# A linear-attention and mixture-of-experts kernel: float32 products on unsplit operands in the attention

## The chip, the cores and the metric

The kernel runs on one core of one Trainium2 chip. The metric is the device time of one execution in microseconds (us); runs of the same kernel here lie within 0.2% of each other.

## The reference, cut to what matters

Three layers in a row, all in float32 (the dense weights arrive as float64 words and are narrowed on the chip):

```python
# attention with a decaying state, 4 batches x 8 heads x 768 tokens x 40 dimensions
m_new = max(f[t] + m, i[t]); f_stab = exp(f[t] + m - m_new); i_stab = exp(i[t] - m_new)
C = f_stab * C + i_stab * outer(v[t], k[t]);  n = f_stab * n + i_stab * k[t]
y[t] = sigmoid(o_gate[t]) * (C @ q[t]) / max(abs(n . q[t]), 1)
x = y as [3072 tokens, 320]
# dense layer: 320 -> 2048 -> 320, leaky relu
x = max(0.01 * (x @ w_in), x @ w_in) @ w_out
# experts: the best of 8 by x @ w_gate, 320 -> 1024 -> 320, times its gates
out[token] = gate[token] * eom[token] * (relu(x @ w1[e]) @ w2[e])
```

The attention is computed in chunks of 128 tokens. Within a chunk the scores (key by query) are multiplied by a matrix of decays; those "probabilities" times v (with a column of ones beside it, 41 columns) give the chunk's own part. The state of 40 x 41 for each head carries the earlier chunks.

## The kernel before, in words

A **unit** is one chunk of one batch with all 8 heads; there are 24, and `unit(i)` emits one as a generator that yields between its stages. In a unit:

1. The raw q, k, v of 128 tokens arrive in `raw` (float32). q and k are split into float16 parts, a high part by ACT's copy and a remainder, and transposed by DMA. For units in `QG` Pool scales q and k in place first and forms the remainder.
2. The decays `gm` (float32) come from TensorE (units 0 to 5) or from a broadcast load with exponentials on ACT (from unit `PEU` = 6 on).
3. For all but the last chunk Pool forms `wv`, v times its weight towards the state; ACT rounds it to float16 (`wvh`) and Pool forms the remainder (`wvl`).
4. v itself is rounded by ACT (`vh`), its remainder is DVE's (`vl`).
5. For each half of the heads four score matmuls fill the one PSUM buffer of tag "S" (L762), DVE multiplies it into `gm`, Pool (ACT for units in `PA`) rounds the product to float16 (`ph`, L768), and Pool (DVE for `LV`) forms the remainder (`pl`).
6. `pv` (L782 to L784) has three float16 matmuls for each head: high times high, high times low, low times high.
7. DVE normalises the result; the gates (`XG`: on Pool, else DVE) and the rounding of x into two float16 parts by `pack` follow (the remainders on Pool for units in `PG`, else on DVE), and a DMA transposes x into `xT`.
8. After each second batch `state` adds both batches' k times `wv` into PSUM (L852: three float16 products for each head and batch, 48 for a pair of units) and updates the state, of which `C3` is a split copy for the next chunk.

**The dense layer** runs in 96 steps, interleaved with the units from about 48 us on: 16 matmuls of 256 columns (L903), ACT and DVE form the leaky relu, ACT and Pool split it into `gh` and `gl`, and 12 matmuls of 320 columns follow (L925 to L927) two steps later. **The experts** follow the last dense step, in blocks of 128 tokens.

**What sets the order.** Each stage has a planned time (`UNITS`, `OFF`, `TICKS`). The class `Order` runs a list schedule by those times, with a cost for each instruction, and fixes the order of the instructions on every engine up to planned time 350. The times are not waited for on the chip: an engine takes its next instruction as soon as the instruction's inputs and its buffer are there, and whatever stands behind a waiting instruction on the same engine waits too. SP issues the loads and the transposes, in order as well. `Bufs` hands scratch buffers round: a load into one waits until its last reader is out. The large weight conversions of the dense layer (`narrow`, `split`: on DVE, ACT and Pool) lie between the first eight units.

Of the kernel before, what the change touches and what calls it, by code (L numbers as in the profile page):

```python
# [20 lines left out]
C = 128  # L21
# [7 lines left out]
PF = 10                      # pairs of tiles from here on share the dense weights' last pass  # L29
TA = 2 * PF                  # token tiles of the first dispatch  # L30
NBA = TA - E + 1             # full blocks that TA tiles always hold
NBH = E // 2                 # first blocks of the rest: up to half a block of two experts each
NBB = NBH + NTILE + E // 2 - 1 - NBA    # blocks of the rest, at most
# [3 lines left out]
S_V = 2.0 ** 5  # L37
S_C = 2.0 ** -4
S_N = 2.0 ** 15
# [25 lines left out]
class Slots:  # L65
    """a tile pool whose tags keep the order of their tiles"""
# [13 lines left out]
class Order:  # L80
    """the order of every engine's instructions: a list schedule by planned time"""
# [61 lines left out]
    def run(self, instrs, planned, pools):  # L143
# [49 lines left out]
        wait = {e: [] for e in self.ENGINES}     # (ready time, i)  # L193
        avail = {e: [] for e in self.ENGINES}    # (priority, i)
# [98 lines left out]
class Bufs:  # L293
    """buffers in turn, each free again once its last reader is out"""
# [12 lines left out]
# the plan: times of the units, of their stages, of the dense steps and of the weights' loads and splits  # L307
UNITS = [2.7, 0, 19, 17.2, 28.8, 32, 42.5, 46.5]
UNITS += [16 + 2.87 * i for i in range(16)]      # from the ninth on in ticks
# [20 lines left out]
# units whose decay between tokens the tensor engine adds up  # L330
PEU = 6
# what the Pool engine takes from the vector engine: packs, reciprocals times gates, gates from these chunks on,
# remainders of queries and keys, of weights
PG = {3, 15, 23}
XG = {0, 2, 5, 8}
# [3 lines left out]
# units whose weights the scalar engine rounds; whose remainders the vector engine takes  # L339
PA = {3, 4, 6}  # L340
LV = {4}
# weights that the scalar engine scales; units with one transpose for query and key
WA = {(2, 0)}
MT = set()
# where blocks begin that few inputs use
RARE = [26, 28]
# the last planned time of a fixed order; lead and queue of the loads
# [5 lines left out]
def emit(tc, gates, qkv, og, w_in, w_out, w_gate, w1, w2, out):  # L353
# [23 lines left out]
    # arena views  # L377
# [44 lines left out]
    maskb = cp.tile([128, C], BF, name="maskb")      # -1e30 where the key is behind the query  # L422
# [47 lines left out]
    def narrow(r):  # L470
        """float64 words -> float32"""
        n = r.shape[1]
        cv = cv64()
        a, b = (x[:, 0:n] for x in cv)
        lo, hi = r[:, :, 0], r[:, :, 1]
        V.tensor_scalar(out=a, in0=hi, scalar1=3, scalar2=0x3FFFFFF8, op0=ALU.logical_shift_left,
                        op1=ALU.bitwise_and)
        yield 0.35
        stt(V, b, hi, -0x40000000, a, ALU.bitwise_and, ALU.bitwise_or)
        yield 0.65  # L480
        stt(V, a, lo, 29, b, ALU.logical_shift_right, ALU.bitwise_or)
        return a.bitcast(F32), cv

    def piece_win(j, blk, lead):
# [8 lines left out]
        else:  # L493
            # two column blocks' last rows: the remainders of each on the other half of the partitions
# [29 lines left out]
    def piece_w2(e, k0, n, until=0.0):  # L524
        """until: the time at which what lay there is used"""
# [24 lines left out]
    raw_r = Bufs([R.f32(2 * DM + H * D1) for _ in range(3)], "raw_r")  # L550
    QK = Bufs([R.f16(2, H, 128) for _ in range(4)], "QK")
    QKT = Bufs([R.f16(2 * H, 128) for _ in range(2)], "QKT")
    VH = Bufs([R.f16(H, 42) for _ in range(2)], "VH")
    VL = Bufs([R.f16(H, 42) for _ in range(2)], "VL")
    GM = Bufs([R.f32(H, C) for _ in range(3)], "GM")
    PH = Bufs([R.f16(4, C) for _ in range(4)], "PH")
    PL = Bufs([R.f16(4, C) for _ in range(4)], "PL")
    WV = Bufs([R.f32(H, D1) for _ in range(2)], "WV")
    WVH = Bufs([R.f16(H, 42) for _ in range(3)], "WVH")
    WVL = Bufs([R3.f16(H, 42) for _ in range(3)], "WVL")  # L560
# [26 lines left out]
    def parts(c):  # L587
        """g and b of chunk c as a sum of three bfloat16 parts, one on each group of 32 partitions"""
# [9 lines left out]
    def arguments(c, h0, tag):  # L598
        """g of the query + b of the key, masked, of four heads: [key, head, query]"""
# [15 lines left out]
    def emit_gates(c0, c1):  # L615
        """gates of chunks c0 to c1: g and b by token, decay of the chunk"""
# [33 lines left out]
        outs = [(gw, wT, S_V)]  # L650
# [19 lines left out]
    def emit_sig(c):  # L670
        """output gates of two chunks"""
        for n in range(2):
            sg[c + n] = SG()
            SP.dma_start(sg[c + n], og[c + n])
        yield SGD
        for n in range(2):
            A.activation(out=sg[c + n], in_=sg[c + n], func=AF.Sigmoid)
            ready.add(c + n)
# [8 lines left out]
    def unit(i):  # L687
        """one (batch, chunk) of all heads"""
# [18 lines left out]
        if i in QG:  # L707
            scaled(G, raw[:, 0:2 * DM], S_QK)
# [12 lines left out]
        else:  # L721
            for a, x in ((qt, qr), (kt, kr)):
                SP.dma_start_transpose(out=a, in_=x.rearrange("p h d -> p (h d)"))
        if i >= PEU:
# [15 lines left out]
        if c < NC - 1:  # L740
            wv, wvh, wvl = WV(), WVH(), WVL()
# [3 lines left out]
            yield 0.7  # L745
            copy(wvh[:, :, 0:D1], wv)
            yield 0.3
            less(True, wvl[:, :, 0:D1], wv, wvh[:, :, 0:D1])
            WV.free(wv)
            st[c, b] = (kr, wvh, wvl, qk)  # L750
        yield to("v")
        vh, vl = VH(), VL()
        copy(vh[:, :, 0:D1], v, S_V)
        low(vl[:, :, 0:D1], v, S_V, vh[:, :, 0:D1])
        raw_r.free(raw)
        pp = []
        for hf in range(2):
# [6 lines left out]
            ph, pl = PH(), PL()  # L764
            if i in PA:
                copy(ph, p32)
            else:
                G.tensor_scalar(out=ph, in0=p32, scalar1=1.0, scalar2=0.0, op0=ALU.mult, op1=ALU.add)  # L768
            yield 0.5
            less(not (i in LV), pl, p32, ph)  # L770
            if hf:
                GM.free(gm)
            pp.append((ph, pl))
# [4 lines left out]
        def pv(hf):  # L778
            ph, pl = pp[hf]
            for h in range(4):  # L780
                g = 4 * hf + h
                T.matmul(o1[:, g, :], ph[:, h, :], vh[:, g, 0:D1], start=True, stop=False)  # L782
                T.matmul(o1[:, g, :], ph[:, h, :], vl[:, g, 0:D1], start=False, stop=False)
                T.matmul(o1[:, g, :], pl[:, h, :], vh[:, g, 0:D1], start=False, stop=True)  # L784

        yield to("p")
        pv(0)
        pv(1)
        PH.free(pp[0][0], pp[1][0])
        PL.free(pp[0][1], pp[1][1])  # L790
        VH.free(vh)
        VL.free(vl)
# [36 lines left out]
        if c == NC - 1:  # L829
            QK.free(qk)  # L830
# [14 lines left out]
    def state(c, pr):  # L845
        up = ps.tile([128, H, D1], F32, tag="aux", name="up", bufs=3)
        for h in range(H):
            for m in range(3):
                for n, o in ((0, 0), (1, 64)):
                    kr, wvh, wvl, _ = st[c, 2 * pr + n]  # L850
                    k0, k1 = ((0, 64), (80, 128), (0, 64))[m] if n == 0 else ((0, 40), (80, 120), (0, 40))[m]
                    T.matmul(up[o:o + k1 - k0, h, :], kr[:, h, k0:k1], (wvh, wvh, wvl)[m][:, h, 0:D1],  # L852
                             start=(m == 0), stop=(m == 2))
        for n in range(2):
            QK.free(st[c, 2 * pr + n][3])
            WVH.free(st[c, 2 * pr + n][1])
            WVL.free(st[c, 2 * pr + n][2])
# [37 lines left out]
    def gemm1(xT, n, kp):  # L895
        """two feed-forward tiles: their leaky relu, split"""
# [54 lines left out]
    late = []           # for the logits of the last tiles, behind the first blocks of experts  # L951

# [1 line left out]
    def routing():  # L954
# [21 lines left out]
        half = [rt([128, E], F32, f"half{i}") for i in range(2)]      # block and row of an expert's half  # L976
# [12 lines left out]
        def dispatch(first, bufs, R1, RS, group):  # L989
            """slots of the blocks: their rows, tokens, scales and experts"""  # L990
# [23 lines left out]
            # scale  # L1014
# [9 lines left out]
            # rank in the expert  # L1024
# [22 lines left out]
            # blocks of the experts  # L1047
# [28 lines left out]
            # block of every token, out of the way for those that the other dispatch holds  # L1076
            def of_expert(i, a, r):
                """a of the expert of every token"""
# [8 lines left out]
            if not first:  # L1087
                # behind the full blocks: half a block
# [9 lines left out]
            # slot -> token  # L1098
# [23 lines left out]
            # row c * 512 + b * 128 + p is token b * 768 + c * 128 + p; none beyond the last  # L1122
# [52 lines left out]
        def experts(q):  # L1175
            """rows of the block and their expert: one for all or a fixed one for each half"""
# [42 lines left out]
        def chain(q0, q1, ahead):  # L1219
            """blocks q0 to q1, each one's second product after the next one's first"""  # L1220
# [105 lines left out]
    for j in range(4):  # L1326
        # these lie where the dense weights of steps up to t lay: two pieces of w_in, then w_out
# [76 lines left out]
```

## Time and profile before

| | us |
|---|---|
| median of 3 runs (lowest, highest) | 726.77 (726.21, 727.49) |
| span of the profiled execution, first to last instruction | 721.0 |
| median less span | 5.8 |
| PE, DVE, ACT, POOL busy | 596.5, 486.8, 369.6, 391.2 |

The page gives only the span for the profiled execution, so its own time is taken as the span and the 5.8 us that the median of the runs lies above it. PE is TensorE's matmuls, PEld its weight loads, DVE VectorE, ACT ScalarE, POOL GpSimd, SP the engine that issues most DMAs. A matmul's recorded duration is a latency: matmuls overlap, so what one costs in a stream is read from the distance of starts.

### The profile page before, as it was taken

What the parts mean: (1) busy time and instruction counts of PE and PEld (TensorE: products, weight loads), DVE (VectorE), ACT (ScalarE), POOL (GpSimd) and SP (SyncE); (2) the same over time, 40 slices, a digit from 0 to 9 for tenths busy, and PEclk for the clock granted to TensorE, in tenths of its full rate; (3) what the DMA queues carried; (4) which work ended last, traced back from release to release, by engine and by line L of the source; (5) the groups of instructions that cost most, each with busy time, mean ns of one, the idle gap of its engine ahead of it and who ended that gap; (6) DMA issues with size and microseconds to landing.
All of it is one profiled execution on the core that took longest, in us unless ns stands there. A gap on an engine that the chain in (4) does not pass through costs nothing. (4 is left out here: it accounts for less than half of the span.)

```text
span 721.0 us, 15741 instructions
## 1 busy us (share of the span) xinstructions
PE 596.5 (83%) x5624; PEld 426.0 (59%) x5624; DVE 486.8 (68%) x871; ACT 369.6 (51%) x772; POOL 391.2 (54%) x392
## 2 busy tenths in 40 slices
PE   3447779769787788977898899999699999999894
PEld 1235557547666566756676687776455655665552
DVE  7999999995588789779698876688635722122110
ACT  5546464677665676777655566655332222222220
POOL 6867887466866858867665544524523422223111
PEclk9997999999999999989999999999899999999997
DMA  8686893681957796987666656544599877777632
GB/s 226 228 150 85 184 259 111 209 215 27 186 159 159 211 237 123 228 185 178 136 161 153 170 153 193 155 129 129 165 198 180 160 155 131 159 151 154 148 88 50
DMA packets 215081, 116.77 MB, mean 162 GB/s; under 512 B 170011, under 2 KB 202523, under 8 KB 215004
## 3 DMA queue, kind: packets, MB, share of 16 engines
q1 hardware_dynamic: 212092, 106.68, 64.6%
q0 software_dynamic: 2912, 9.05, 4.5%
q8 instruction: 50, 0.82, 0.5%
q14 instruction: 27, 0.22, 0.1%
HBM read 64.58 MB, written 9.06 MB: 102 GB/s over the span
## 5 line engine op out<-in xcount | busy, mean ns | idle before, releaser
L903 PE MATMUL hp<-xT,arena 128*128 128x256 f16 x1536 | 197.2, 279 | 8.8 <-DVE g L366 7.8
L366 POOL TENSOR_TENSOR gl<-g,gh 128x512 f16<-128x512 f32 x96 | 131.8, 1374 | 111.1 <-ACT gh L375 108.7
L903 PEld LDWEIGHTS <-arena 128*128 128x128 f16 x1536 | 148.3, 100 | 31.5 <-issue 5.7
L925 PE MATMUL acc<-arena,gh 128*128 128x320 f16 x384 | 117.3, 307 | 14.3 <-DVE arena L1276 4.8
L927 PE MATMUL acc<-arena,gl 128*128 128x320 f16 x384 | 117.1, 308 | 9.9 <-POOL gl L366 9.8
L366 POOL TENSOR_TENSOR arena<-arena 128x512 f16<-128x512 f32 (+5 forms) x94 | 111.2, 1195 | 18.5 <-ACT arena L375 10.2
L926 PE MATMUL acc<-arena,gh 128*128 128x320 f16 x384 | 117.4, 306 | 0.5 <-POOL arena L366 0.5
L363 DVE SCALAR_TENSOR_TENSOR r<-hp,r 128x512 f16<-128x512 f32 x52 | 35.9, 691 | 120.8 <-ACT r L1194 106.5
L363 DVE SCALAR_TENSOR_TENSOR arena<-arena 128x328 f16<-128x328 f32 (+7 forms) x113 | 99.1, 888 | 9.3 <-ACT arena L375 7.1
L1188 PE MATMUL hp<-arena,xbb 128*128 (+1 forms) x480 | 95.5, 382 | 5.9 <-issue 5.6
L375 ACT ACTIVATE gh<-g 128x512 f16<-128x512 f32 x96 | 60.1, 626 | 70.3 <-DVE g L366 67.6
L366 DVE TENSOR_TENSOR g<-hp,t 128x512 f32<-128x512 f32 x96 | 65.2, 680 | 41.6 <-ACT t L375 36.0
L1207 PE MATMUL y<-arena,rT 128*128 (+1 forms) x720 | 90.4, 299 | 0.8 <-DMA rT<-r 0.5
L375 ACT ACTIVATE arena<-arena 128x328 f16<-128x328 f32 (+5 forms) x128 | 72.9, 599 | 33.3 <-DVE arena L363 12.7
L1207 PEld LDWEIGHTS <-rT 128*128 128x128 f16 (+1 forms) x720 | 61.8, 101 | 28.0 <-DMA rT<-r 1.4
L1211 POOL DMA_INDIRECT out<-ys,si x26 | 26.8, 1030 | 90.2 <-ACT ys L1210 83.3
L1188 PEld LDWEIGHTS <-xbb 128*128 128x128 f16 (+1 forms) x480 | 41.5, 102 | 53.1 <-issue 10.7
L375 ACT ACTIVATE t<-hp 128x512 f32<-128x512 f32 x96 | 56.1, 585 | 30.0 <-PE hp L903 29.9
L363 DVE SCALAR_TENSOR_TENSOR arena<-stg,arena 128x960 f16<-128x960 f32 (+3 forms) x48 | 57.5, 1198 | 15.3 <-ACT arena L375 14.9
L1194 ACT ACTIVATE r<-hp 128x512 f16<-128x512 f32 x52 | 31.0, 597 | 65.5 <-PE hp L1188 49.3
L375 ACT ACTIVATE arena<-stg 128x1024 f16<-128x1024 f32 (+2 forms) x48 | 46.9, 978 | 17.6 <-DMA stg<-w 10.6
L1169 POOL DMA_INDIRECT xbb<-x2rows,gi x26 | 28.0, 1077 | 49.0 <-PE hp L1188 42.9
(242 smaller groups left out, 855.3 us busy)
## 6 DMA issues: line engine op xcount, KB each, us to landing
stg<-w SPq DMA_DIRECT2D x24, 512.0 KB
arena<-qkv SPq DMA_DIRECT2D x24, 484.0 KB
arena<-gd SPq DMA_DIRECT2D x18, 512.0 KB
stg<-w SPq DMA_DIRECT2D x16, 480.0 KB
raw<-w_in SPq DMA_DIRECT2D x10, 512.0 KB
arena<-w_out SPq DMA_DIRECT2D x8, 640.0 KB
x2rows<-x2r SPq DMA_DIRECT2D x24, 192.0 KB
arena<-og SPq DMA_DIRECT2D x6, 640.0 KB
```

Of the source, the lines that this page charges most:

```text
L363: eng.scalar_tensor_tensor(out=o, in0=a, scalar=s, in1=b, op0=op0, op1=op1)
L366: eng.tensor_tensor(out=o, in0=a, in1=b, op=op)
L375: A.activation(out=o, in_=a, func=AF.Copy, scale=s)
L903: T.matmul(hp[:, kk, :], win_v[:, j, wb, o:o + 128], xT[:, xb, :], start=(m == 0), stop=(m == 7))
L925: T.matmul(acc[i], gh[:, kk, r], wh, start=(k == lo), stop=False)
L926: T.matmul(acc[i], gh[:, kk, r], wl, start=False, stop=False)
L927: T.matmul(acc[i], gl[:, kk, r], wh, start=False, stop=(k == hi))
L1169: G.indirect_dma_start(out=xb, out_offset=None, in_=rows, in_offset=bass.IndirectOffsetOnAxis(ap=gi[:, i:i + 1], axis=0), bounds_check=(TA ...
L1188: T.matmul(hp[n][r], xT[:, xb, r], W1v[:, e, wb, n * 512:(n + 1) * 512].rearrange("p a b -> p (a b)"), start=(m == 0), stop=(m == 7))
L1194: A.activation(out=r[:, 0, :], in_=hp[n], func=AF.Relu)
L1207: T.matmul(y[r], a[:, r], W2v[:, e, k, m, :].rearrange("p a b -> p (a b)"), start=(k + n == 0), stop=(k == 7 and n == 2))
L1211: G.indirect_dma_start(out=out, out_offset=bass.IndirectOffsetOnAxis(ap=D_[s][1][:, i:i + 1], axis=0), in_=ys, in_offset=None, bounds_chec ...
```

## The change

The float16 splits of the probabilities, of v and of the weighted v go away; the products that used them become one float32 matmul for each head. k for the state is taken from the raw load, so `raw` lives until the state's product and q and k may no longer be scaled in place (`QKS` takes the scaled copy). Pool takes the gates (`XG`) and the remainders of x (`PG`) of all units. Scales and numbers of buffers follow. The planned times stay as they are.

```diff
-S_V = 2.0 ** 5
-S_C = 2.0 ** -4
-S_N = 2.0 ** 15
+S_W = 2.0 ** 5
+S_C = 2.0
+S_N = S_QK * S_QK
-PG = {3, 15, 23}
-XG = {0, 2, 5, 8}
+PG = set(range(24))
+XG = set(range(24))
-PA = {3, 4, 6}
-LV = {4}
...
-    raw_r = Bufs([R.f32(2 * DM + H * D1) for _ in range(3)], "raw_r")
-    QK = Bufs([R.f16(2, H, 128) for _ in range(4)], "QK")
+    raw_r = Bufs([R.f32(2 * DM + H * D1) for _ in range(6)], "raw_r")
+    QKS = R.f32(2 * DM)
+    QK = Bufs([R.f16(2, H, 128) for _ in range(2)], "QK")
...
-    GM = Bufs([R.f32(H, C) for _ in range(3)], "GM")
-    PH = Bufs([R.f16(4, C) for _ in range(4)], "PH")
-    PL = Bufs([R.f16(4, C) for _ in range(4)], "PL")
-    WV = Bufs([R.f32(H, D1) for _ in range(2)], "WV")
-    WVH = Bufs([R.f16(H, 42) for _ in range(3)], "WVH")
-    WVL = Bufs([R3.f16(H, 42) for _ in range(3)], "WVL")
+    GM = Bufs([R.f32(H, C) for _ in range(4)], "GM")
+    WV = Bufs([R.f32(H, D1) for _ in range(4)], "WV")
...
         if i in QG:
-            scaled(G, raw[:, 0:2 * DM], S_QK)
+            G.tensor_scalar(out=QKS, in0=raw[:, 0:2 * DM], scalar1=S_QK, scalar2=0.0, op0=ALU.mult, op1=ALU.add)
+            q, k = (QKS[:, u * DM:(u + 1) * DM].rearrange("p (h d) -> p h d", h=H) for u in range(2))
...
+        QK.free(qk)
...
-            wv, wvh, wvl = WV(), WVH(), WVL()
+            wv = WV()
             tt(G, wv, v, w.to_broadcast([128, H, D1]), ALU.mult)
-            yield 0.7
-            copy(wvh[:, :, 0:D1], wv)
-            yield 0.3
-            less(True, wvl[:, :, 0:D1], wv, wvh[:, :, 0:D1])
-            WV.free(wv)
-            st[c, b] = (kr, wvh, wvl, qk)
-        yield to("v")
-        vh, vl = VH(), VL()
-        copy(vh[:, :, 0:D1], v, S_V)
-        low(vl[:, :, 0:D1], v, S_V, vh[:, :, 0:D1])
-        raw_r.free(raw)
+            st[c, b] = (raw, wv)
...
             tt(V, p32, sc, p32, ALU.mult)
-            ph, pl = PH(), PL()
-            if i in PA:
-                copy(ph, p32)
-            else:
-                G.tensor_scalar(out=ph, in0=p32, scalar1=1.0, scalar2=0.0, op0=ALU.mult, op1=ALU.add)
-            yield 0.5
-            less(not (i in LV), pl, p32, ph)
...
-                T.matmul(o1[:, g, :], ph[:, h, :], vh[:, g, 0:D1], start=True, stop=False)
-                T.matmul(o1[:, g, :], ph[:, h, :], vl[:, g, 0:D1], start=False, stop=False)
-                T.matmul(o1[:, g, :], pl[:, h, :], vh[:, g, 0:D1], start=False, stop=True)
+        for h in range(H):
+            T.matmul(o1[:, h, :], gm[:, h, :], v[:, h, :], start=True, stop=True)
+        GM.free(gm)
+        if c == NC - 1:
+            raw_r.free(raw)
...
         for h in range(H):
-            for m in range(3):
-                for n, o in ((0, 0), (1, 64)):
-                    kr, wvh, wvl, _ = st[c, 2 * pr + n]
-                    k0, k1 = ((0, 64), (80, 128), (0, 64))[m] if n == 0 else ((0, 40), (80, 120), (0, 40))[m]
-                    T.matmul(up[o:o + k1 - k0, h, :], kr[:, h, k0:k1], (wvh, wvh, wvl)[m][:, h, 0:D1],
-                             start=(m == 0), stop=(m == 2))
+            for n, o in ((0, 0), (1, 64)):
+                raw, wv = st[c, 2 * pr + n]
+                k0 = DM + h * D
+                T.matmul(up[o:o + 64 - 24 * n, h, :], raw[:, k0:k0 + 64 - 24 * n], wv[:, h, :], start=True, stop=True)
```

## Rows read from the trace of the kernel before

**Rows 1.** Busy time by stage, columns: stretch, length, engines (instructions), clock, DMA.
```profile
0.00:162.00 162.00, 104.85 (x1071) 75.73 (x1072) 151.42 (x228) 92.74 (x190) 115.77 (x134) 0.94 0.75 186
162.00:414.00 252.00, 210.64 (x2448) 166.81 (x2447) 199.21 (x329) 167.04 (x387) 173.75 (x164) 0.97 0.71 165
414.00:522.70 108.70, 99.87 (x855) 77.94 (x852) 80.48 (x159) 62.44 (x107) 49.31 (x41) 0.98 0.54 155
522.70:721.00 198.30, 181.16 (x1260) 105.47 (x1258) 55.65 (x156) 47.43 (x89) 52.32 (x54) 0.97 0.72 143
```
**Rows 2.** DVE's groups by line, 0 to 162 us: busy us, mean ns | idle before.
```profile
L363 DVE SCALAR_TENSOR_TENSOR arena<-arena 128x328 f16<-128x328 f32 x9 | 7.0, 776 | 0.2
...
L366 DVE TENSOR_TENSOR arena<-arena,rd 128x320 f32<-128x320 f32 x5 | 4.9, 988 | 0.1
L363 DVE SCALAR_TENSOR_TENSOR xr<-arena,xr 128x256 f16<-128x256 f32 x7 | 3.7, 524 | 0.0
...
L363 DVE SCALAR_TENSOR_TENSOR xr<-arena,xr 128x128 f16<-128x128 f32 x7 | 3.1, 437 | 0.0
```
**Rows 3.** DVE's groups by line, 162 to 414 us.
```profile
L363 DVE SCALAR_TENSOR_TENSOR arena<-arena 128x328 f16<-128x328 f32 x15 | 12.1, 805 | 1.7 <-ACT arena L375 1.7
...
L363 DVE SCALAR_TENSOR_TENSOR xr<-arena,xr 128x256 f16<-128x256 f32 x14 | 11.6, 829 | 4.4 <-ACT xr L375 4.4
...
L366 DVE TENSOR_TENSOR arena<-arena,rd 128x320 f32<-128x320 f32 x14 | 9.5, 681 | 0.2
...
L363 DVE SCALAR_TENSOR_TENSOR xr<-arena,xr 128x128 f16<-128x128 f32 x14 | 8.0, 569 | 1.7 <-ACT xr L375 1.6
```
**Rows 4.** Groups by line of the whole span, POOL's.
```profile
L366 POOL TENSOR_TENSOR arena<-arena 128x512 f16<-128x512 f32 x48 | 63.9, 1337 | 2.7 <-ACT arena L375 1.1
...
L768 POOL TENSOR_SCALAR arena<-arena 128x512 f16<-128x512 f32 x42 | 30.4, 724 | 15.3 <-DVE arena L366 14.5 <-DVE rd L366 0.7
...
L366 POOL TENSOR_TENSOR arena<-arena 128x328 f16<-128x328 f32 x20 | 20.2, 1017 | 6.0 <-ACT arena L375 5.8
...
L366 POOL TENSOR_TENSOR arena<-arena,rd 128x320 f32<-128x320 f32 x4 | 3.4, 860 | 3.6 <-DVE rd L810 2.4 <-DVE arena L366 1.1
...
L366 POOL TENSOR_TENSOR xr<-arena,xr 128x256 f16<-128x256 f32 x3 | 2.5, 844 | 3.4 <-ACT xr L375 3.4
...
L366 POOL TENSOR_TENSOR xr<-arena,xr 128x128 f16<-128x128 f32 x3 | 1.3, 423 | 0.0
```
**Rows 5.** The waits of PE, 162 to 414 us: total, times, longest.
```profile
PE sc L762 <- DVE arena L366: 16.4, 10, 4.0
...
PE o L784 <- POOL arena L366: 6.0, 7, 1.8
```
**Rows 6.** Timeline of PE, one unit's products with the probabilities: start, us.
```profile
197.72 0.18 PE L782 MATMUL o<-arena 128*128 128x41 f16 x1
...
198.33 0.27 PE L903 MATMUL hp<-xT,arena 128*128 128x256 f16 x1
```
**Rows 7.** Timeline of PE, the state of one pair of units, and what follows.
```profile
209.58 0.89 PE L852 MATMUL up<-arena 128*64 128x41 f16 x48
210.40 0.50 PE L903 MATMUL hp<-xT,arena 128*128 128x256 f16 x3
```
**Rows 8.** Timeline of PE: three, then all four float32 transposes of the gates.
```profile
67.47 0.37 PE L661 MATMUL pt<-ident,arena 32*128 32x32 f32 x3
...
67.47 0.43 PE L661 MATMUL pt<-ident,arena 32*128 32x32 f32 x4
67.83 0.31 PE L927 MATMUL acc<-arena,gl 128*128 128x320 f16 x1
```
**Rows 9.** Groups by line of the whole span, DVE's operations of 8 columns.
```profile
L807 DVE TENSOR_SCALAR rd<-arena 128x8 f32<-128x8 f32 x20 | 11.3, 564 | 0.1
...
L807 DVE TENSOR_SCALAR rd<-o 128x8 f32<-128x8 f32 x4 | 0.6, 143 | 0.0
```
**Rows 10.** The waits of SP's queue, 0 to 162 us: total, times, longest.
```profile
SPq L828 <- DVE rd L807: 11.7, 1, 11.7
```

More of the change, by code (lines that the diff above doesn't have):

```diff
@@ L549, in emit @@
     cv64 = Bufs([(R64.f32(640).bitcast(I32), R64.f32(640).bitcast(I32)) for _ in range(2)], "cv64")
-    raw_r = Bufs([R.f32(2 * DM + H * D1) for _ in range(3)], "raw_r")
-    QK = Bufs([R.f16(2, H, 128) for _ in range(4)], "QK")
+    raw_r = Bufs([R.f32(2 * DM + H * D1) for _ in range(6)], "raw_r")
+    QKS = R.f32(2 * DM)
+    QK = Bufs([R.f16(2, H, 128) for _ in range(2)], "QK")
     QKT = Bufs([R.f16(2 * H, 128) for _ in range(2)], "QKT")
-    VH = Bufs([R.f16(H, 42) for _ in range(2)], "VH")
-    VL = Bufs([R.f16(H, 42) for _ in range(2)], "VL")
-    GM = Bufs([R.f32(H, C) for _ in range(3)], "GM")
-    PH = Bufs([R.f16(4, C) for _ in range(4)], "PH")
-    PL = Bufs([R.f16(4, C) for _ in range(4)], "PL")
-    WV = Bufs([R.f32(H, D1) for _ in range(2)], "WV")
-    WVH = Bufs([R.f16(H, 42) for _ in range(3)], "WVH")
-    WVL = Bufs([R3.f16(H, 42) for _ in range(3)], "WVL")
+    GM = Bufs([R.f32(H, C) for _ in range(4)], "GM")
+    WV = Bufs([R.f32(H, D1) for _ in range(4)], "WV")
     CS = [R.f32(H, D1, p=104) for _ in range(B // 2)]
@@ L649, in emit_gates @@
         yield GW
-        outs = [(gw, wT, S_V)]
+        outs = [(gw, wT, S_W)]
         if c0:
@@ L744, in unit @@
             tt(G, wv, v, w.to_broadcast([128, H, D1]), ALU.mult)
-            yield 0.7
-            copy(wvh[:, :, 0:D1], wv)
-            yield 0.3
-            less(True, wvl[:, :, 0:D1], wv, wvh[:, :, 0:D1])
-            WV.free(wv)
-            st[c, b] = (kr, wvh, wvl, qk)
-        yield to("v")
-        vh, vl = VH(), VL()
-        copy(vh[:, :, 0:D1], v, S_V)
-        low(vl[:, :, 0:D1], v, S_V, vh[:, :, 0:D1])
-        raw_r.free(raw)
-        pp = []
+            st[c, b] = (raw, wv)
         for hf in range(2):
@@ L763, in unit @@
             tt(V, p32, sc, p32, ALU.mult)
-            ph, pl = PH(), PL()
-            if i in PA:
-                copy(ph, p32)
-            else:
-                G.tensor_scalar(out=ph, in0=p32, scalar1=1.0, scalar2=0.0, op0=ALU.mult, op1=ALU.add)
-            yield 0.5
-            less(not (i in LV), pl, p32, ph)
-            if hf:
-                GM.free(gm)
-            pp.append((ph, pl))
             if hf == 0:
@@ L776, in unit @@
         o1 = ps.tile([128, H, D1], F32, tag="aux", name="o1", bufs=3)
[L778 to L781, printed above, removed]
-                T.matmul(o1[:, g, :], ph[:, h, :], vh[:, g, 0:D1], start=True, stop=False)
-                T.matmul(o1[:, g, :], ph[:, h, :], vl[:, g, 0:D1], start=False, stop=False)
-                T.matmul(o1[:, g, :], pl[:, h, :], vh[:, g, 0:D1], start=False, stop=True)
-        yield to("p")
[L787 to L792, printed above, removed]
+        yield to("p")
+        for h in range(H):
[3 more added lines that the diff above has]
+            raw_r.free(raw)
         yield to("c")
@@ L828, in unit @@
         SP.dma_start_transpose(out=xTs[i // 2][:, :, j * 128:(j + 1) * 128], in_=xr)
-        if c == NC - 1:
-            QK.free(qk)
         if c < NC - 1 and b % 2:
@@ L847, in state @@
         for h in range(H):
-            for m in range(3):
-                for n, o in ((0, 0), (1, 64)):
-                    kr, wvh, wvl, _ = st[c, 2 * pr + n]
-                    k0, k1 = ((0, 64), (80, 128), (0, 64))[m] if n == 0 else ((0, 40), (80, 120), (0, 40))[m]
-                    T.matmul(up[o:o + k1 - k0, h, :], kr[:, h, k0:k1], (wvh, wvh, wvl)[m][:, h, 0:D1],
-                             start=(m == 0), stop=(m == 2))
+            for n, o in ((0, 0), (1, 64)):
+                raw, wv = st[c, 2 * pr + n]
+                k0 = DM + h * D
+                T.matmul(up[o:o + 64 - 24 * n, h, :], raw[:, k0:k0 + 64 - 24 * n], wv[:, h, :], start=True, stop=True)
         for n in range(2):
-            QK.free(st[c, 2 * pr + n][3])
-            WVH.free(st[c, 2 * pr + n][1])
-            WVL.free(st[c, 2 * pr + n][2])
+            raw_r.free(st[c, 2 * pr + n][0])
+            WV.free(st[c, 2 * pr + n][1])
         yield 2.0
```

## Prediction

> **What bounds the kernel now.** I read the busy times by stage first, then the groups by line of each stage, then the waits of TensorE, and last the timeline of the products that are replaced. The reader is to see four stages [rows 1]. Up to 162 us DVE is the bound: 151.4 of 162 us, 93%, while PE records 104.9, 65%. From 162 to 414 us no engine is full: PE 210.6 of 252 (84%), DVE 199.2 (79%), ACT 167, POOL 174 (69%); the fixed order on each engine makes them wait for one another. From 414 us the attention is over and PE has 99.9 of 108.7; then come the experts, 198 us, mostly PE. The last two stages hold nothing that is edited. They begin when the last dense step ends, so a gain or loss in the first two stages moves them as they are.
>
> What PE waits for in the second stage is the next thing to see [rows 5]: 16.4 us at L762, where a score matmul waits for DVE to empty the one "S" buffer, and 6.0 us at L784, where a product with the probabilities waits for Pool's remainder `pl`.
>
> **What the change takes from Pool, ACT and DVE.** Pool loses 42 roundings `ph` (30.4 us), 46 of 48 remainders of its 512-column group (`pl`; the other two belong to weights) at 1.337 us, 61.5, and 20 remainders `wvl` (20.2): 112 us. It gains 21 pairs of remainders of x at 0.844 + 0.423 us, 26.6, and 20 gates at 0.860, 17.2: 44 us. Net it has 68 us less [rows 4]. ACT loses 24 `vh`, 20 `wvh` and six `ph`. I cost that at nothing: ACT is busy 57 and 66% in the two stages [rows 1] and stands before Pool's or DVE's longer work; without that cover it would be a small gain, no loss.
>
> DVE loses `vl`, the gates and the remainders of x. In the first stage that is 7.0 + 4.9 + 3.7 + 3.1 = 18.7 us [rows 2]; in the second 12.1 + 9.5 + 11.6 + 8.0 = 41.2 us [rows 3], 21% of its 199.2.
>
> **What it does to TensorE: the unknown price.** A unit's 24 float16 products with the probabilities take 198.33 - 197.72 = 0.61 us, 25 ns each [rows 6]. The state of a pair takes 210.40 - 209.58 = 0.82 us for 48 [rows 7]. They become 8 and 16 float32 products, of 41 columns. The trace has no such product. The nearest rows are the gates' float32 transposes, 32 columns wide: the fourth adds 0.43 - 0.37 = 0.06 us to three, and from the first to the next float16 matmul pass 0.36 us, 0.12 more than four times 0.06 [rows 8]. So float16 work does not overlap with the end of such a group; I count 0.2 us for a group's two ends.
>
> - Lower end: 0.06 us by the columns, 41/32, is 0.08 us.
> - Upper end: a transpose only moves its operand, while a float32 product may be put together from four products of halves. Four of the transposes' 0.06 are 0.24 us.
> - I take four products at the float16 price, 4 x 25 = 102 ns. It lies between the ends, nearer to the rows, and says that an unsplit product costs one more piece than the three of before.
>
> At 0.102 us a unit's products take 8 x 0.102 + 0.2 = 1.02 us, 0.41 more; a pair's state 16 x 0.102 + 0.2 = 1.83 us, 1.0 more. The first stage holds 8 units and 4 states: 3.3 + 4.0 = 7.3 us. The second holds 16 and 6: 6.6 + 6.0 = 12.6 us.
>
> The Trainium skill ("TensorE: Matmul & The Clock Gate", section "Terms") says that a transpose mode makes float32 four times faster. If L661's transposes run in it, an ordinary float32 product costs four of them; no row here shows which mode they run in. That is the upper end, and the sum by it is the first rival's.
>
> **The sum.** First stage: DVE's 18.7 us count by its share of 93%, 17.5 us; PE's 7.3 us more count by PE's share of 65%, 4.7. It ends 12.8 us earlier. Second stage: the 6.0 us at L784 go, since the products now wait for DVE's multiplication alone. Of the 16.4 us at L762 I take half, 8.2: DVE has 21% less to do, and what waits in a queue shrinks faster than its load. That gains 14.2 us; PE's 12.6 us more count by its 84%, 10.5. Net 3.7 us earlier. Together 16.5 us: the profiled span of 721.0 becomes 704.5, and with the 5.8 us that the median lies above the span, **710 us**.
>
> **What is moved, and costs nothing.** The gates and remainders of x go from DVE past Pool's queue, behind `gl` of a dense step; what waits for them is the transpose of x on SP, and behind it SP's loads and other transposes. Pool's net loss of work covers it; without that a unit's x would come some 2.1 us later (0.860 + 0.844 + 0.423) [rows 4]. `raw` is now kept until the state's product, so a load of q, k and v on SP waits for PE instead of for DVE. Six buffers instead of three stand against that, and units of the second stage come some 16 us apart (252 us for 16). `QK` has two buffers instead of four, but is free once it is transposed. `QKS` is one buffer, written and last read by Pool in order. No load is added. After the change DVE's multiplication into `gm` is what the products with the probabilities wait for, and PE itself is the next thing late.
>
> **The rivals.**
>
> *TensorE becomes the bound (slower).* At 0.24 us for a product a unit takes 2.12 us, 1.51 more, and a state 4.04, 3.22 more: 25 us in the first stage and 43.5 in the second. The second stage would hold 210.6 + 43.5 = 254 us of PE work in 252 us, so all of it counts: 43.5 - 14.2 = 29 us later. In the first, (104.9 + 25) / (162 - 17.5) = 90% of 25 us stands against the 17.5: 5 us later. Together 34 us: **761 us**. Between the two prices the sum changes sign at about 0.147 us. For it speaks that an operand of 32 bits holds more than the two float16 parts that take three products now; against it, that the only float32 rows stand at 0.06 us. The Trainium skill ("FP8 and Floating Point Precision", section "TensorE Precision Notes") says that true float32 takes four passes through the array; by that rule this rival is the one to expect if each pass costs what a transpose of this trace costs, and my value if it costs a float16 product.
>
> *Pool's lighter load also speeds up DVE.* DVE's operation on 8 columns takes 564 ns with its operand in the scratch memory and 143 ns early on with it in the accumulator [rows 9]: 0.42 us in which DVE seems to be held up. Pool has 68 of the 289.5 us that it is busy before 414 us taken away, 24%. If half of the 200 instructions that DVE keeps in the first stage (228 [rows 1] less 28 [rows 2]) gain a quarter of 0.42 us, that is 10 us, and some 3 more at L762: **697 us**.
>
> *The DVE time is hidden anyway.* SP waits up to 11.7 us for one transpose of x [rows 10], with loads queued behind it. If that queue, or Pool's place in it now, sets the first stage, the 17.5 us are not gained and only the second stage's 3.7 stand against PE's 4.7: **728 us** at most, no change.
>
> **How the numbers follow.** About 0.2% is what a measurement of this kernel can tell from no change. The forecast (704 us, with products at 0.08, to 716) has a chance of 0.40, the faster rival 0.18, no gain 0.10, PE as the bound 0.32. Faster is 0.40 + 0.18 = 0.58; of the 0.10 and of the passage through zero near 0.147 us I give 0.08 to the same; slower is 0.34. The range from 693 to 750 leaves out the far parts of the fast rival (under 0.1) and of the slow one (0.1). Held to the forecast alone it is 704 to 716.
>
> **What the profile after would show.** Right: DVE some 62 us less busy and Pool 68 less; the first stage's end, when PE first runs full, near 149 us; no wait of a product with the probabilities for Pool; the starts of float32 products about 0.1 us apart. Wrong: starts 0.2 us or more apart and PE's waits for DVE gone without the dense steps coming sooner; or SP waiting for PE with loads behind it. Most of the doubt is in that one distance.

## The result, and the profile after

The changed kernel takes 699.5 us (median of 4 runs, 697.2 to 700.5) against 727.1 us: a ratio of 0.961 (95% interval 0.959 to 0.963), 27.6 us less. The prediction was 710 us, 693 to 750. In the spans it is 721.0 against 695.4, 25.6 us less, where the sum had said 16.5.

The first part of the page of the changed kernel (busy time of each engine in us, share of the span, instructions):
```profile
PE 616.7 (89%) x5272; PEld 455.7 (66%) x5272; DVE 414.0 (60%) x783; ACT 350.6 (50%) x722; POOL 315.3 (45%) x344
```
DVE is 72.8 us less busy (some 62 were counted), Pool 75.9 less (68), PE 20 us more. Then the busy times by stage, in the stretches of [rows 1]:
```profile
0.00:162.00 162.00, 125.81 (x1042) 97.03 (x1043) 127.74 (x206) 94.22 (x193) 99.31 (x125) 0.97 0.78 189
162.00:414.00 252.00, 236.94 (x2349) 195.80 (x2347) 167.83 (x289) 162.84 (x364) 129.37 (x137) 0.99 0.74 176
```
DVE no longer fills the first 162 us (79% for 93%), and PE records 94% of the second stretch, where it had 84%.

Where the time went is read from landmarks: the first and last start of three lines, first in the kernel before (the last integer conversion of the dense weights on DVE, the score matmuls, the first product of the experts; ns are shortest, median, longest):
```profile
L476 DVE TENSOR_SCALAR arena<-arena x8: 478/482/1375, 20.7 to 150.8; 128x640 int32<-128x640 int32 x8
...
L762 PE MATMUL sc<-arena x192: 216/218/314, 17.9 to 398.5; 120*128 120x128 f16 x192
...
L1188 PE MATMUL hp<-arena,xbb x480: 376/379/635, 522.9 to 703.0; 128*128 x118, 128*64 128x512 f16 x42
```
and the same lines in the changed kernel:
```profile
L473 DVE TENSOR_SCALAR arena<-arena x8: 435/489/1333, 17.8 to 133.1; 128x640 int32<-128x640 int32 x8
...
L745 PE MATMUL sc<-arena x192: 216/218/314, 16.6 to 373.1; 120*128 120x128 f16 x192
...
L1148 PE MATMUL hp<-arena,xbb x480: 376/379/634, 501.5 to 676.8; 128*128 x118, 128*64 128x512 f16 x42
```
The weights' conversion ends 17.7 us earlier, the attention's last scores 25.4, so 7.7 more in the second stage; the experts begin 21.4 us earlier (the dense steps that are left over give 4.0 back), and the end comes 25.6 us earlier, 4.2 more among the experts.

PE's waits from 162 to 414 us, to be read beside [rows 5]:
```profile
PE lp L908 <- DMA x2T<-x2r: 11.3, 11, 3.4
PE sc L745 <- DVE arena L363: 2.8, 2, 2.3
```
The 6.0 us for Pool are gone, the 16.4 us for DVE have become 2.8.

Last, the price that was in doubt. A float32 product leaves two matmuls in the trace. The products with the probabilities are 24 x 8 = 192 in the changed kernel and have 384 records, where L782, one of the three float16 lines of the kernel before, has 192 records for 192 products:
```profile
L782 PE MATMUL o<-arena 128*128 128x41 f16 x192 | 21.0, 185 | 2.9 <-POOL arena L768 2.9
```
```profile
L753 PE MATMUL o<-arena 128*128 128x41 f32 x384 | 49.7, 290 | 0.3 <-DVE arena L363 0.3
```
In PE's timeline the 16 records are therefore one unit's eight products, and the 32 are the 16 state products of one pair of units, each shown with what follows:
```profile
198.09 1.88 PE L753 MATMUL o<-arena 128*128 128x41 f32 x16
199.80 0.37 PE L763 MATMUL o<-arena 120*128 120x41 f16 x8
...
222.92 1.13 PE L814 MATMUL up<-arena 128*64 128x41 f32 x32
223.98 0.72 PE L863 MATMUL hp<-xT,arena 128*128 128x256 f16 x5
```
A unit's products take 199.80 - 198.09 = 1.71 us, 0.21 us each, where the 24 float16 products took 0.61 us [rows 6]. A pair's state takes 223.98 - 222.92 = 1.06 us, 0.07 us a product, where it took 0.82 us [rows 7]. The granted clock is 1.00 at both places.

### The profile page after: what moved, and what is told of

Read it like the earlier page. It is cut to its first block, busy times and chain, and to the rows that moved or that the text cites. A ratio compares the mean times of both kernels' runs of the same rounds, so it can differ in the third digit from the quotient of the medians.

```text
span 695.4 us, 14848 instructions
## 1 busy us (share of the span) xinstructions
PE 616.7 (89%) x5272; PEld 455.7 (66%) x5272; DVE 414.0 (60%) x783; ACT 350.6 (50%) x722; POOL 315.3 (45%) x344
## 5 line engine op out<-in xcount | busy, mean ns | idle before, releaser
L863 PE MATMUL hp<-xT,arena 128*128 128x256 f16 x1536 | 193.5, 278 | 8.6 <-DVE g L363 6.4
L363 POOL TENSOR_TENSOR gl<-g,gh 128x512 f16<-128x512 f32 x96 | 127.0, 1323 | 136.6 <-ACT gh L372 131.0
L885 PE MATMUL acc<-arena,gh 128*128 128x320 f16 x384 | 116.0, 303 | 4.5 <-ACT arena L372 2.1
L886 PE MATMUL acc<-arena,gh 128*128 128x320 f16 x384 | 116.3, 303 | 0.0
L360 DVE SCALAR_TENSOR_TENSOR arena<-arena 128x320 f16<-128x320 f32 (+6 forms) x89 | 75.1, 854 | 15.1 <-ACT arena L372 12.5
L372 ACT ACTIVATE arena<-arena 128x640 f16<-128x640 f32 (+3 forms) x78 | 51.3, 673 | 36.2 <-DVE arena L360 13.7
L1171 POOL DMA_INDIRECT out<-ys,si x26 | 26.4, 1017 | 88.7 <-ACT ys L1170 81.0
L887 PEld LDWEIGHTS <-gl 128*128 128x128 f16 x384 | 37.7, 99 | 24.8 <-POOL gl L363 10.5
L753 PE MATMUL o<-arena 128*128 128x41 f32 x384 | 49.7, 290 | 0.3 <-DVE arena L363 0.3
```

The lines of the kernel that those rows point to most:

```text
L360: eng.scalar_tensor_tensor(out=o, in0=a, scalar=s, in1=b, op0=op0, op1=op1)
L363: eng.tensor_tensor(out=o, in0=a, in1=b, op=op)
L372: A.activation(out=o, in_=a, func=AF.Copy, scale=s)
L753: T.matmul(o1[:, h, :], gm[:, h, :], v[:, h, :], start=True, stop=True)
L863: T.matmul(hp[:, kk, :], win_v[:, j, wb, o:o + 128], xT[:, xb, :], start=(m == 0), stop=(m == 7))
L885: T.matmul(acc[i], gh[:, kk, r], wh, start=(k == lo), stop=False)
```

## The experiments

Twelve kernels ran, all timed beside the kernel before; a ratio is to that kernel's runs on the same chip. The changed kernel stands at 0.961, from the runs of the section above, and was not timed again beside these twelve. The kernel before has medians from 723.2 us (beside the experiments up to the doubled products, but for the one without remainders) to 727.1 us (above), and its runs of one set lie up to 1.0% apart, not 0.2%. So a difference of up to some 4 us between an experiment and the changed kernel can't be told from that shift; where it matters, both the ratio and the time are given.

**The moved part alone.** The kernel before with

```diff
-PG = {3, 15, 23}
-XG = {0, 2, 5, 8}
+PG = set(range(24))
+XG = set(range(24))
```


> The kernel before with only the moved part: Pool forms the gates and the remainders of x of all units, the products stay float16. Theory 'DVE binds the first stage': DVE loses 41 us in all, 12 of them before 162 us, Pool gains 44 us and is then at about 75% in the first and 80% in the second stage; 714 to 719 us against 727. Rival 'Pool's relief is what pays, and Pool's queue now lies on the way of x': 725 to 735 us.

Measured: 1.012 (1.008 to 1.016), 8 us slower. The first theory fell. Its first stage in the busy times:
```profile
0.00:162.00 162.00, 94.27 (x959) 65.93 (x960) 139.39 (x204) 90.16 (x190) 128.96 (x149) 0.79 0.70 181
```
Pool is at 129 us of 162 and PE falls to 94, at a mean granted clock of 0.79 where the kernel before has 0.94 [rows 1]. DVE is lighter by 12 us, and the stage is not shorter: the last integer conversion starts at 155.9 us, where it was 150.8. Taking work off DVE onto Pool does not pay while Pool also has the probabilities. Whether Pool's queue or the lower clock makes the loss is not separated.

**The products alone.** The changed kernel with `PG` and `XG` as before.

> The changed kernel with the sets of before for the gates and the remainders of x: only the float32 products and the splits that fall away with them. Theory: DVE loses 20 us, Pool 112, the products cost 0.5 us a unit; most of the gain stays, 706 to 713 us. Rival 'the moves carry the gain': 718 us or more. If the two parts add up, its gain and that of the moves alone make 27 us together.

Measured: 0.969 (0.965 to 0.972), 22.6 us less. The products carry the gain. The moves, which cost 1.2% alone, bring 2.1 us on top of them by the times (701.6 and 699.5) and 0.8% by the ratios, which is too little to tell from the shift of the kernel before. The two parts do not add up: 3.1% less and 1.2% more would be 1.9% less, and it is 3.9%.

**Pool given back its work.** The kernel of the run before, and Pool does again what the products took from it, into buffers that nobody reads:

```diff
             tt(V, p32, sc, p32, ALU.mult)
+            if i not in {3, 4, 6}:
+                G.tensor_scalar(out=SA, in0=p32, scalar1=1.0, scalar2=0.0, op0=ALU.mult, op1=ALU.add)
+            if i != 4:
+                less(True, SB, p32, SA)
...
+            less(True, SB.rearrange("p h t -> p (h t)")[:, 0:H * D1], wv.rearrange("p h d -> p (h d)"),
+                 raw[:, 2 * DM:])
```


> The float32 products with the gates and remainders of x as before, and Pool given back what the products took from it (the roundings and remainders of the probabilities, the remainders of the weighted v: 112 us), written into two spare buffers that nobody reads. Theory 'Pool's lighter load is what pays' (its queue is shorter and DVE's operations run faster beside it: 0.82 instead of 1.0 us for the 512-column integer ones): 715 to 725 us, DVE's operations as slow as in the kernel before. Rival 'what pays is DVE's, ACT's and the shorter wait of the products': within 4 us of the products alone, 697 to 706 us.

Measured: 0.998 (0.995 to 1.000). Nearly all of the 3.1% is gone, though PE, ACT, the products and the numbers of buffers are those of the kernel that had it. So neither the products nor the added buffers make the gain by themselves.

**Pool filled with writes.** The same place, but four fills of a spare buffer (`G.memset(SA, 0.0)`) for each half.

> As the run before, but Pool's spare time is filled with four fills of 512 columns for each half of the probabilities, which read nothing. If Pool slows DVE by being busy or late at all: as slow as with the work given back. If it slows DVE by reading the same memory: DVE's operations stay as fast as with the products alone, and the time lies in the lower half between 700 and 720 us.

Measured: 0.979 (0.977 to 0.981): a third of the gain gone, 1.0 of 2.9 points. The first part of the page, for the products alone:
```profile
PE 623.6 (89%) x5272; PEld 461.4 (66%) x5272; DVE 434.1 (62%) x845; ACT 350.2 (50%) x722; POOL 275.4 (39%) x282
```
with the work given back:
```profile
PE 628.9 (87%) x5272; PEld 463.5 (64%) x5272; DVE 474.4 (66%) x845; ACT 350.0 (49%) x722; POOL 388.2 (54%) x390
```
and with the fills:
```profile
PE 617.0 (88%) x5272; PEld 458.1 (65%) x5272; DVE 433.9 (62%) x845; ACT 350.8 (50%) x722; POOL 370.2 (53%) x474
```
The reader is to see DVE: the same 845 instructions take 40 us more beside Pool's work and not a microsecond more beside Pool's fills, with Pool about as busy in both. The group that changes most is (DVE's 32 remainders of q, k and weights of 320 columns; busy us, mean ns), with the products alone, then with the work, then with the fills:
```profile
L360 DVE SCALAR_TENSOR_TENSOR arena<-arena 128x320 f16<-128x320 f32 x32 | 21.7, 680 | 9.5 <-ACT arena L372 9.3
```
```profile
L360 DVE SCALAR_TENSOR_TENSOR arena<-arena 128x320 f16<-128x320 f32 x32 | 28.9, 907 | 5.6 <-ACT arena L372 5.5
```
```profile
L360 DVE SCALAR_TENSOR_TENSOR arena<-arena 128x320 f16<-128x320 f32 x32 | 22.1, 692 | 12.5 <-ACT arena L372 12.5
```
Not every group does this. DVE's 96 operations of 512 columns that read the accumulator (`g` from `hp`) take 684, 683 and 684 ns, the 20 integer ones of 512 columns 820, 889 and 955 ns, and the 8-column operation of [rows 9] 322, 324 and 327 ns.

So about a third of what Pool's relief is worth comes back with fills that only take Pool's time; the other two thirds go with Pool's operations that read and compute, beside which DVE takes 40 us more. That this slowing alone makes the two thirds is not shown, for the fills differ in two more ways. They do not hold `gm` or `wv`, so buffers may be free earlier. And they read nothing and need not wait for DVE: Pool sits idle for 26.4 us before its roundings in the first run and for 6.4 us before the fills in the second.

**Pool's relief without the change of products.** The kernel before without the remainders of the probabilities: `pl` is filled with zeros once, `less(not (i in LV), pl, p32, ph)` is left out, so the output lacks that part.

> The kernel before with the remainders of the probabilities left out: they are filled with zeros once, all float16 products run as before, so the output lacks that part. Pool has 61 us less to do, PE exactly the same. Theory 'Pool's relief pays, not the kind of product': 112 us of Pool given back cost 21 us, so 61 us should be worth 8 to 14 us, 710 to 716 against 723. Rival 'it takes the shorter chain of the products themselves, or the buffers': within 4 us of before.

Measured: 0.983 (0.979 to 0.987), 12.5 us less, inside the first theory's 8 to 14. PE's 5624 instructions are the same; Pool is 59 us less busy and DVE, with two instructions fewer, 25 us:
```profile
PE 591.9 (83%) x5624; PEld 422.9 (59%) x5624; DVE 462.1 (65%) x869; ACT 368.1 (51%) x772; POOL 331.9 (46%) x350
```
The products here no longer wait for Pool's remainder either, 6.0 us of PE's waits before [rows 5]; how much of the 12.5 us that makes is not separated.

**DVE given back its remainder of v.** The changed kernel with

```diff
+        stt(V, SA, raw[:, 2 * DM:], S_W, raw[:, 2 * DM:], ALU.mult, ALU.subtract)
```
in every unit. 

> The changed kernel with DVE given back one operation of 328 columns a unit, as the remainder of v was (24 of 0.8 us, 19 us; nine of them before 162 us), into a spare buffer. Theory 'DVE binds the first stage': 6 to 8 us from the first stage and some 2 from the second, 706 to 711 us. Rival 'DVE's load no longer counts': within 3 us of 699.

Measured: 0.968 (0.965 to 0.971) and 700.3 us: 5 us more than the changed kernel by the ratios, 0.8 us more by the times. DVE is 10 us busier. So DVE's own load costs at most about a quarter of the 19 us that were expected of the operations, and it is not settled that it costs anything.

**What a float32 product costs.** The changed kernel with the products made in halves,

```diff
-            T.matmul(o1[:, h, :], gm[:, h, :], v[:, h, :], start=True, stop=True)
+            for n in (0, 64):
+                T.matmul(o1[n:n + 64, h, :], gm[:, h, n:n + 64], v[:, h, :], start=True, stop=True)
```


> The changed kernel with each product with the probabilities made in two halves of 64 queries, whose outputs lie on the two halves of the partitions. Theory 'a float32 product costs two loads of its stationary columns' (2 x 128 at 2.4 GHz are 107 ns, 112 measured; the state's products, 64 and 40 columns on two halves of the partitions, take 63 ns for a pair): 60 to 65 ns for a head instead of 112, 9 us less of PE in all, 691 to 696 us. Rival 'a fixed price of four passes at 25 ns or more each': a head stays at 112 ns or takes up to 224, 699 to 715 us.

and with 82 moving columns instead of 41,

```diff
+            n = min(h + 2, H)
+            T.matmul(o9[:, h:n, :].rearrange("p h d -> p (h d)"), gm[:, h, :],
+                     v[:, h:n, :].rearrange("p h d -> p (h d)"), start=True, stop=True)
```


> The changed kernel with seven of a unit's eight products with the probabilities made 82 columns wide instead of 41; the second half of each result is overwritten by the next product. Theory 'the stationary loads set the price': still 107 to 115 ns apart, time within 2 us of the changed kernel's. Rival 'the moving columns set it, at four clocks each': 82 x 4 / 2.4 = 137 ns or more, 5 us more in all.

Measured, PE's timeline of one unit with the halves and what follows:
```profile
171.27 1.13 PE L754 MATMUL o<-arena 128*64 128x41 f32 x32
172.34 0.37 PE L764 MATMUL o<-arena 120*128 120x41 f16 x8
```
and with the wide products:
```profile
198.03 1.88 PE L755 MATMUL o<-arena 128*128 128x82 f32 x16
199.74 0.37 PE L766 MATMUL o<-arena 120*128 120x41 f16 x8
```
Both expectations took the distance of two records, 112 ns, for the price of a product, which is two records. Eight heads in halves take 1.07 us, 0.13 us a head, where whole products take 0.21. Twice the moving columns change nothing: 1.71 us for eight products in both. So the moving columns do not set the price here. The halves have fewer stationary columns and their outputs on two halves of the partitions; which of the two makes them cheaper was not separated.

The times: 0.964 (0.958 to 0.970) with the halves, no better than the changed kernel although PE is 12.5 us less busy; 0.975 (0.969 to 0.982) with the wide ones, in two runs, 7 us slower by the times and 10 by the ratios at the same price of a product. The cost by which the list schedule orders the instructions counts columns, so the wide products also changed the order on the engines; that the order is the cause is likely and not shown. In the kernel with the halves PE's waits from 162 to 414 us are
```profile
PE sc L745 <- DVE arena L363: 14.0, 8, 3.8
PE lp L909 <- DMA x2T<-x2r: 8.7, 10, 1.7
```
What PE saved it waits for at DVE: 14.0 us where the changed kernel has 2.8.

**Every product with the probabilities twice.** `for _ in range(2):` ahead of the changed kernel's matmul.

> The changed kernel with each product with the probabilities issued twice: 192 more products at 112 ns, 21.5 us more of PE, 14 of them in the second stage. Theory 'PE is the bound of the second stage': 14 to 20 us more, 713 to 720 us. Rival 'PE has slack, since halving the price of these products gained nothing': under 7 us more, 699 to 706 us.

Measured: 1.026 (1.023 to 1.030), 47 us more than the changed kernel by the ratios, 43 by the times: both theories missed. Here too the expectation counted one record, 112 ns, as a product. At the full clock a unit's 16 products, 32 records, take 3.49 us (230.15 to 233.64 us) where eight took 1.71, so 24 units have some 43 us more. The last integer conversion starts 16.3 us later than in the changed kernel and the last scores 42.0 us later. PE's timeline at one place:
```profile
252.42 4.90 PE L754 MATMUL o<-arena 128*128 128x41 f32 x32
```
and the busy times around it (the columns as in [rows 1]):
```profile
252.40:257.40 5.00, 5.00 (x47) 5.00 (x44) 0.00 (x0) 0.92 (x2) 0.00 (x1) 0.74 1.03 287
257.40:261.40 4.00, 4.00 (x24) 2.50 (x21) 2.76 (x8) 0.75 (x2) 0.72 (x1) 0.50 0.99 286
```
For 4.9 us PE runs nothing but float32 products back to back, recorded as fully busy; within them the granted clock falls to half, and the float16 work of the next 4 us runs at 1.2 GHz. DVE is idle for 6.1 us there: it waits for the matmul (L764) that stands behind these products on PE. Of the 16 units from 162 us on, the clock falls in or just behind the products of five (at 217.2, 254.8, 316.2, 350.4 and 408.4 us), four times with no gap between PE's records before it; behind the others it stays. In the changed kernel each fall between 60 and 500 us follows waits of PE that add up to 2 us or more. So PE's added work comes back almost whole in the time: PE had little slack left. What the lower clock adds and what slack took up were not measured.

**Three tries at a better version.** The logits' matmuls planned 8 us behind their transpose instead of 3 (`yield 8.0` in `x2out`):

> The changed kernel with the logits planned 8 us behind their transpose instead of 3: in the second stage PE waits 10.5 us, ten times, at the logits' matmuls for that transpose, by far its longest wait left. Theory 'PE's waits are what is left to gain there': 4 to 9 us less, 690 to 695. Rival 'PE's order gives it back elsewhere': within 2 us of 699.

The same with the halves, and four more of the dense weights' remainders on Pool (`WG` with (1, 0), (1, 1), (3, 0), (3, 1) added):

> The halved products, the later logits, and four more of the dense weights' remainders on Pool instead of DVE (Pool is at 61% before 162 us, DVE at 79%). If DVE is still the first stage's bound: 5 to 8 us more than the later logits give, 684 to 690. If Pool's extra reading slows DVE by what it sheds: no better than the later logits alone, 692 to 700.

And the halves and the later logits without those weights:

> The halved products and the later logits together, without the moved weights. If PE is the second stage's bound once its waits are gone, the 9 us that the halves take from PE now count: 3 to 6 us under the later logits alone, 688 to 692 us (0.950 to 0.955 of before). Rival 'PE's own work is not what binds, and each change of the order scatters by some us': 0.955 to 0.965.

Measured: 0.957 (0.952 to 0.961), 0.965 (0.961 to 0.969) and 0.962 (0.958 to 0.966). The first is the lowest of all, but its interval overlaps the changed kernel's 0.959 to 0.963, so it is not shown to be faster. More weights on Pool did not pay, as in the rival expected there. PE's shorter products again gained nothing.

## Why the prediction was right, and where its sum was not

- **Direction and size.** 710 was forecast, 699.5 measured, inside 693 to 750 but below the 704 to 716 of the sum. The time lies nearest to the faster rival, 697, and what that rival rests on, that Pool's lighter load speeds up DVE, is what the runs bear out; how much of the gain goes through DVE's speed is not separated.
- **What Pool's load is worth** is a term that was mis-sized. The sum gave Pool's 68 us the 6.0 us of PE's waits at L784 and nothing else, and put the gain on what DVE loses. Given back 112 us of its work, Pool takes back 20.8 us of 22.6; without 59 us of it, the kernel before gains 12.5. Some 40 us of DVE's busy time hang on it with the same instructions. The rival's own sign was not a good one: the operation on 8 columns fell from 564 to 322 ns with the products alone, but with Pool's work given back it stayed at 324. Nor do the 36 integer operations that are neither removed nor moved show it: 38.7 us before, 33.8 in the changed kernel, and 34.5 with Pool's work given back.
- **The first stage** was to end 12.8 us earlier and ends 17.7. DVE was 93% busy there, but lighter work on DVE paid only once Pool was light: the moves alone made the stage no shorter.
- **The second stage**: 3.7 forecast, 7.7 measured, though PE's new products cost more there than was counted. The wait at L762 fell by 13.6 us in this stretch, not by half of 16.4.
- **The price of a product with the probabilities** is the other term that was mis-sized. 1.02 us a unit was counted and 1.71 is measured, so 1.10 more than before and not 0.41. 0.21 us a product lies past the 0.147 at which the sum was to change sign, and near the slow rival's 0.24. Four pieces at the float16 price give half of it; the upper end, four of the transposes' 0.06 us, is nearest. Of the signs of being wrong, starts of products 0.2 us or more apart did come; but the dense steps came sooner all the same. The rule that float32 takes four passes (the Trainium skill, "FP8 and Floating Point Precision", section "TensorE Precision Notes") is not contradicted, since passes are not seen; 0.21 us is some 3.5 times a transpose.
- **The price of the state** was mis-sized the other way: 1.83 us a pair of units, 1.0 more than before, was forecast; 1.06 us is measured, 0.24 more. That is 7.7 us of PE over the ten pairs.
- **What the sum makes of both prices.** The first stage has 8 x 1.10 + 4 x 0.24 = 9.8 us more of PE, the second 16 x 1.10 + 6 x 0.24 = 19.0. By the shares of the prediction the first stage gains 17.5 - 6.4 and the second loses 16.0 - 14.2, together 9.3 us less: 717 us, outside the sum's own range. The time came out lower than 710 all the same; by the experiments it is Pool's relief, left to a rival, that was worth more than the dear products cost. That the two errors partly cancel is luck.
- **The moved work's place** behind Pool's queue cost nothing, as was said, but only in the changed kernel; with the moves alone, where Pool has no net loss of work, the kernel is 1.2% slower. That fits "Pool's net loss of work covers it".
- **The last two stages** were to move as they are. They gave back 4.0 and gained 4.2. Among the experts PE waits less without a cause that the profile shows (the first row is before, the second after, both from 480 us on):
```profile
PE hp L1188 <- issue: 5.6, 8, 0.9
```
```profile
PE hp L1148 <- issue: 2.4, 4, 0.8
```
  The code of this stage is the same; why it waits less stays open.
- **What lies around the span.** The 5.8 us were taken from a median of other executions. The profiled run of the changed kernel took 697.2 us at a span of 695.4, 1.8 us more, so a part of the 5.8 was scatter between executions.

## What to carry to other kernels

An engine that is not the bound can still set the bound's speed: before pricing an edit by what the fullest engine loses, look whether its operations run longer beside another engine's, by comparing the same group with that engine busy and idle, and give that a price. One group of [rows 9] was not enough for it. Work taken from one engine and put on a second is judged with what the second has to do already: the same move cost 1.2% with Pool full and cost nothing that could be seen with Pool light. Before a price is read from starts in a timeline, count the records that one call of the program leaves: here 16 records were eight products, and the price was twice the distance of two records. Making the dear products cheaper gained nothing here and doubling them cost 43 to 47 us: what a saving is worth depends on what PE waits for next.

## What the runs showed of the hardware

- A float32 product is recorded as two matmuls. Eight of them with 128 stationary columns took 1.71 us at 2.4 GHz, 0.21 us each, with 41 or 82 moving columns alike; 24 float16 products in their place had taken 0.61 us. Sixteen with 64 stationary columns and outputs on alternate halves of the partitions took 1.07 us, 0.07 us each.
- Sixteen float32 products back to back, with PE recorded as busy throughout, did not always keep the clock: it fell from 2.4 to 1.2 GHz in or just behind them in 5 of 16 units. In the changed kernel, with eight in a row, each fall between 60 and 500 us followed 2 us or more of waits.
- DVE's operations slowed down beside Pool's operations that read and compute (845 instructions 474.4 us for 434.1; one group 907 ns for 680) and not beside Pool's fills (433.9 us; 692 ns). Those of 512 columns that read the accumulator did not (684 and 683 ns).
